# A planned list order that looks ahead on VectorE and ScalarE, and block sums issued in pieces

## The chip, the core and the metric

The kernel runs on one core of a Trainium2 chip. A core has TensorE (matrix products into the eight banks of PSUM, 128 partitions x 512 float32 each), VectorE and ScalarE (elementwise work, both can read and write PSUM), GpSimd, and SyncE, whose queue issues all DMAs of this kernel. The profile calls them PE (PEld for its weight loads), DVE, ACT, POOL and SP. The metric is the device time of one execution in microseconds; the time before is the median of three runs.

## The reference

Two blocks read the same normalised x. One is linear attention with 32 heads, the other a gated feed-forward net; the output is x plus the product of the first with silu of the second.

```python
def _A_ref(x, wqkv, wo):
    B, S, D = x.shape                # 1, 2048, 1024
    H = 32; Dh = D // H
    qkv = (lambda x, *d: x.transpose(*d))((x @ wqkv).reshape(B, S, 3, H, Dh), 2, 0, 3, 1, 4)
    q, k, v = qkv[0], qkv[1], qkv[2]
    phi = lambda t: jnp.where(t > 0, t + 1, jnp.exp(t)) + 1e-6
    pq, pk = phi(q), phi(k)
    kv = jnp.einsum("bhsd,bhse->bhde", pk, v)
    z = jnp.einsum("bhsd->bhd", pk)
    num = jnp.einsum("bhqd,bhde->bhqe", pq, kv)
    den = jnp.einsum("bhqd,bhd->bhq", pq, z)[..., None] + 1e-6
    o = num / den
    return (lambda x, *d: x.transpose(*d))(o, 0, 2, 1, 3).reshape(B, S, D) @ wo

def _B_ref(x, w_gate, w_up, w_down):
    g = _silu(x @ w_gate)            # w_gate, w_up: 1024 x 3584
    u = x @ w_up
    return (g * u) @ w_down

x = A_x
xn = _layernorm(x, axis=-1)
s = _A_ref(xn, A_wqkv, A_wo)
g = _silu(_B_ref(xn, B_w_gate, B_w_up, B_w_down))
return x + s * g
```

## The kernel before

**The products.** Nearly every product is a Strassen-Winograd product: the operands are cut into 2 x 2 blocks, and seven block products (numbered 1 to 7 in `Set.step`) do the work of eight. For that, sums and differences of blocks are needed on both sides. On the moving side they are called T1 = R01 - R00, T2 = R11 - T1, T3 = R11 - R01 and T4 = R10 - T2 (T1 is written over R01, so T3 comes first); products 5, 6, 7 and 4 read T1, T2, T3 and T4. On the stationary side the four sums are numbered 5, 6, 7 and 3. These block sums are VectorE subtractions of 16-bit data in SBUF, written with `tt(..., True)` (line 360). The change is about how they are cut:

- `combos` (line 459 on): T3, T1, T2, T4 of the weights for k and v (`KVV[0]`, `KVV[1]`) and of x (`XV[0]`, `XV[1]`), each one operation of 2048 elements a partition;
- `m_sum`: the same for the attention matrix `MV`, the four sums of 2048;
- `wd_sum`: T1 to T4 of the down weights, each as two halves of 3584;
- `Group.mk`: the sums of h in the down projection. There are four groups of 512 rows (`Group`). A group holds four blocks of h in slots of 14 pair blocks of 256 columns; `sum5`, `sum67` and `sum3` make four sums of them. Group 0 is loaded and summed in two cuts, pair blocks 0 to 11 and 12 to 13 (3072 and 512 elements), the others in one of 3584.

Around each step stand the evacuations: `put1` and `put5` copy a bank with ScalarE (`act`, line 350), products 6 and 7 add a copy to a bank with VectorE (line 360). `phi_evac` makes phi of a k or q block: the exponential on ScalarE, min and add on VectorE (L734, `tensor_scalar`), then max and add reading PSUM or SBUF (L735, `scalar_tensor_tensor`), which frees the bank.

**The stages.** First x is loaded, normalised by tile of 128 rows (`ln_tile`: statistics L647 and L651, aggregate L652, L653, a power on GpSimd L656, L664, then the scaled copy) and transposed. Tiles 0 and 1 go through `p_piece(tile, w, column half)`, plain products of eight matmuls of 512 columns with the weights of k (w = 0) and v (w = 1); three banks are held for kv sums and two for transposes in this time, so the pieces take turns in three banks. The order of the pieces is k of tile 0 (halves 1, 0), k of tile 1 (1, 0), v of tile 0 half 1, v of tile 1 half 1, v of tile 0 half 0, v of tile 1 half 0. Then come k and v of the other tiles as Strassen sets with the key-value sums (`a_tile`) in between; then q, gate and up by token half p = 0, 1 (`q_pair`, `gu_pair`), with the joint small products of products 1 and 5 cut once more (`inner_stat`, `inner_move`); the attention output (`s_pair`) between; h goes out to a scratch in DRAM (`h_done`); at last the down projection with h read back (`Group.load`), and the output.

**The order of the work** isn't written out: `Plan` collects every operation with its reads, writes, its cost in the plan and its preceding operations, and `schedule` makes a list order for each engine. Costs in the plan: an operation of VectorE takes its elements / 960 + 0.07 (16-bit: / 1920, some others more), so 0.603 for 1024 16-bit elements; a matmul of 512 columns 0.216; every result is there 0.25 to 0.3 us after its operation; a DMA has a rate and two fixed parts. An operation is due (`dl`) at what TensorE has to do before it in program order plus 30, or earlier, when a successor is due: its successor's due time less its own cost and latency. `schedule` plays this plan through: each engine that is free takes, of the operations that are ready in the plan, the one due first, or, where none is ready, the one that is ready first. TensorE takes the first in program order within a window of six. `emit` then writes each engine's list, with semaphore waits where a preceding operation is on another engine or on the same one (not for TensorE behind TensorE). On the chip each engine follows its list strictly: an operation whose data are late holds up all behind it.

Of the kernel before, what the change touches and what calls it, by code (L numbers as in the profile page):

```python
# [10 lines left out]
ALU = mybir.AluOpType  # L11
# [19 lines left out]
class Plan:  # L31
# [59 lines left out]
    def schedule(self):  # L91
        ops = self.ops
        for o in reversed(ops):
            d = o.pecum if o.eng == "pe" else o.pecum + 30.0
            for s in o.succs:
                extra = (4.0 + o.nbytes / 200e3) if o.sem is not None else o.busy + o.lat
                d = min(d, s.dl - extra)
            o.dl = d - o.urgent
        pes = [o for o in ops if o.eng == "pe"]
        cum = [o.pecum + o.busy for o in pes]  # L100
        for o in ops:
            if o.sem is not None and o.succs:
                k = bisect_right(cum, o.dl - self.lead) - 1
                if k >= 0 and pes[k] not in o.preds:
                    o.preds.add(pes[k])
                    pes[k].succs.append(o)
        for o in ops:
            o.npred = len(o.preds)
            o.ready = 0.0
        free = {e: 0.7 for e in self.ENGS}  # L110
        dma_free = 0.0
        table = ACT.Exp
        avail = {e: [] for e in self.ENGS}
        pe_next = deque(o for o in ops if o.eng == "pe")
        for o in ops:
            if o.npred == 0:
                avail[o.eng].append(o)
        order = []
        done = set()
        total = len(ops)  # L120
        while len(order) < total:
            best = None
            for e in self.ENGS:
                a = avail[e]
                if not a:
                    continue
                t = free[e]
                if e == "pe":
                    lim = None
                    n = 0  # L130
                    for o in pe_next:
                        if n >= self.window:
                            lim = o.idx
                            break
                        n += 1
                    cand = [o for o in a if lim is None or o.idx < lim]
                    if not cand:
                        continue
                    rdy = [o for o in cand if o.ready <= t + 0.05]
                    o = min(rdy, key=lambda o: o.idx) if rdy else min(cand, key=lambda o: (o.ready, o.idx))  # L140
                else:
                    rdy = [o for o in a if o.ready <= t]
                    o = min(rdy, key=lambda o: (o.dl - o.boost + self.SWITCH * (o.tab not in (None, table)), o.idx)
                            ) if rdy else min(a, key=lambda o: (o.ready, o.dl))
                s = max(t, o.ready)
                if best is None or s < best[0]:
                    best = (s, e, o)
            s, e, o = best
            o.start = s
            if o.sem is not None:  # L150
                free[e] = s + 0.08
                t0, rate, t1 = self.ALONE if o.start < self.RUSH else self.MIXED
                b = max(s + t0, dma_free)
                dma_free = b + o.nbytes / rate
                o.done = dma_free + t1
            else:
                busy = o.busy
                if o.tab not in (None, table):
                    table = o.tab
                    busy += self.SWITCH  # L160
                free[e] = s + busy
                o.done = s + busy + o.lat
            avail[e].remove(o)
            if e == "pe":
                done.add(o)
                while pe_next and pe_next[0] in done:
                    pe_next.popleft()
            order.append(o)
            for q in o.succs:
                q.npred -= 1  # L170
                q.ready = max(q.ready, o.done)
                if q.npred == 0:
                    avail[q.eng].append(q)
        self.order = order
        return order
# [55 lines left out]
def build_kernel(nc, A_x, A_wqkv, A_wo, B_w_gate, B_w_up, B_w_down, out, WINDOW=6, NWARM=14, NPE=4, LEAD=12.0):  # L231
# [12 lines left out]
    with ExitStack() as es:  # L244
# [98 lines left out]
        def nel(ap):  # L343
            n = 1
            for s in ap.shape[1:]:
                n *= s
            return n
# [8 lines left out]
        def dve(reads, writes, fn, n, rate=0.96):  # L356
            return PL.op("dve", reads, writes, fn, n / (rate * 1000.0) + 0.07)

        def tt(reads, writes, o, a, b, op, fast=False):
            return dve(reads, writes, lambda h: h.tensor_tensor(o, a, b, op), nel(o), 1.92 if fast else 0.96)  # L360
# [79 lines left out]
        def xview(arena, base=0):  # L440
            d = {}
            for nm, b in (("R00", 0), ("R10", 1), ("T1", 2), ("R11", 3), ("T2", 4), ("T3", 5), ("T4", 6)):
                d[nm] = xblock(arena, b, base)
            d["R01"] = d["T1"]
            return d

        XV = [xview(X), xview(P)]
        MV = xview(H, 16 * KB)

        def combos(v):  # L450
            tt([v["R11"][1], v["R01"][1]], [v["T3"][1]], v["T3"][0], v["R11"][0], v["R01"][0], ALU.subtract, True)
            tt([v["R01"][1], v["R00"][1]], [v["T1"][1]], v["T1"][0], v["R01"][0], v["R00"][0], ALU.subtract, True)
            tt([v["R11"][1], v["T1"][1]], [v["T2"][1]], v["T2"][0], v["R11"][0], v["T1"][0], ALU.subtract, True)
            tt([v["R10"][1], v["T2"][1]], [v["T4"][1]], v["T4"][0], v["R10"][0], v["T2"][0], ALU.subtract, True)


        wz = TM.at(0, 1 * KB, FP16)
# [2 lines left out]
        for n in range(NWARM):  # L460
            b = n % 8
# [207 lines left out]
        R01 = (H, 12 * KB)  # L669
# [173 lines left out]
        p_piece(0, 1, 1)  # L843
        t_tile(2)
        combos(KVV[0])
        p_piece(1, 1, 1)
        ln_tile(3)
        p_piece(0, 1, 0)
        t_tile(3)
        combos(KVV[1])  # L850
        p_piece(1, 1, 0)
        for b in tb:
# [50 lines left out]
        for q, kb in enumerate(kvb):  # L903
            n = 3 if q < 2 else 2
# [291 lines left out]
        MIN = {}  # L1196

        def m_sum(o, a, b):
            tt([MV[a][1], MV[b][1]], [MV[o][1]], MV[o][0], MV[a][0], MV[b][0], ALU.subtract, True)

        def s_pair(g):
            p, j0 = g // 2, g % 2
# [49 lines left out]
        def wv(nm, h):  # L1252
            vs, rs, _ = DV["T1" if nm == "R01" else nm]
            v = vs[h]
            return (v.bitcast(BF16) if nm[0] == "R" else v), rs[h]

        def wd_sum(o, a, b):
            for h in range(2):
                (ov, orr), (av, ar), (bv, br) = wv(o, h), wv(a, h), wv(b, h)
                tt([ar, br], [orr], ov, av, bv, ALU.subtract, True)  # L1260

        DIN = {}
        DAT = (tuple((W, q * 3584) for q in range(3)), ((W, 28 * KB), (W, 28 * KB + 3584), (W, 43 * KB)))
# [19 lines left out]
        def hv(s, n0=0, n1=NPAIR):  # L1283
            return (s.ap(FP16).rearrange("p (n t) -> p n t", t=256)[:, n0:n1], s.sub(n0 * 512, (n1 - n0) * 512).r)

        class Group:
# [11 lines left out]
                        h_scr[self.g, i, k][:, n0:n1, :], dsem("hl%d_%d" % (s.k, c)), (n1 - n0) * 64 * KB)  # L1298

            def mk(self, o, a, b, op):  # L1300
                for n0, n1 in self.cuts:
                    (ov, orr), (av, ar), (bv, br) = hv(o, n0, n1), hv(a, n0, n1), hv(b, n0, n1)
                    tt([ar, br], [orr], ov, av, bv, op, True)

# [58 lines left out]

        XV[1]["R01"] = xblock(R01[0], 0, R01[1])
        combos(XV[0])
        combos(XV[1])
        XIN[1] = inner_move(XV[1], 4, in_places(W, 6 * KB, KB))
# [28 lines left out]
        def s_first():  # L1396
            raw, cmb = raw_ring.take(), cmb_ring.take()
            for nm, (sl, o) in (("T2", (raw, 0)), ("T3", (raw, 4)), ("T4", (cmb, 0))):
                MV[nm] = xblock(sl.a, 0, sl.off + o * KB)
            m_sum("T2", "R11", "T1")  # L1400
            m_sum("T3", "T2", "R00")
            m_sum("T4", "R10", "T2")
            MIN.update(inner_move(MV, 4, (tuple((cmb.a, cmb.off + (4 + q) * KB) for q in range(3)),)))
            MIN.update(inner_move(MV, 4, (tuple((H, (40 + q) * KB) for q in range(3)),), ms=(5,)))
            sp[0] = s_pair(0)
# [36 lines left out]
        G[0].sum67()  # L1442
        feed(None)
        wd_sum("T2", "R11", "T1")
        wd_sum("T3", "T2", "R00")
        wd_sum("T4", "R10", "T2")
        for g, c in enumerate(G):
            n = G[g + 1] if g < 3 else None
# [73 lines left out]
def bass_recurrent_scan__linear_attn_block__swiglu_ffn__prompt_kernel(  # L1522
    nc: bass.Bass,
    A_x: bass.AP,
    A_wqkv: bass.AP,
    A_wo: bass.AP,
    B_x: bass.AP,
    B_w_gate: bass.AP,
    B_w_up: bass.AP,
    B_w_down: bass.AP,  # L1530
    out: bass.AP,
):
    build_kernel(nc, A_x, A_wqkv, A_wo, B_w_gate, B_w_up, B_w_down, out)
# [28 lines left out]
```

## Time and profile before

| | |
|---|---|
| median of 3 runs | 719.88 us (719.76 to 720.52) |
| the profiled execution's own time | 719.0 us |
| its span, first to last instruction | 717.2 us |
| granted TensorE clock | 1.00 in all parts |
| HBM read, written | 61.87 MB, 23.20 MB |

The times that follow are from the profiled execution and count from the start of its span. In a row of the timeline stand start, duration, engine, line, operation, what it writes and reads, and how often; in square brackets the idle time of the engine before it and what ended that. In a row of groups stand the number of operations, their busy time, the mean length of one in ns and the idle time before them. A row of waits has the total, the number and the longest in us. In a row of stretches stand its length and then the busy time (and number of instructions) of PE, PEld, DVE, ACT and POOL, the granted clock, the share of the DMA engines and GB/s. Neighbouring instructions of VectorE overlap by a little, so that durations add up to more than the time from start to start.

### The profile page before, as it was taken

The page shows a single profiled execution, that of the slowest core. Times are in us where ns is not written, and L with a number is a line of the kernel's source. Part 1 is how long each engine was busy: PE and PEld are TensorE (multiplying, and loading weights), DVE is VectorE, ACT ScalarE, POOL GpSimd, SP SyncE. Part 2 cuts the span into 40 slices and gives each one's busy share as a digit, 9 for nine tenths or more (in the row PEclk, how much of TensorE's full clock was granted, in tenths as well). Part 3 has the DMA queues.
Part 4 walks back from the last instruction along what each step waited for, and adds up shares of the span by engine and source line. Part 5 has one row for each costly group of instructions (what it writes and reads, how often), then busy time and mean ns, then how long its engine had stood idle before and what let it go on. Part 6 is the DMA issues. An engine that isn't in the chain of part 4 may idle for free.

```text
span 717.2 us, 10813 instructions
## 1 busy us (share of the span) xinstructions
PE 707.3 (99%) x4064; PEld 385.4 (54%) x4064; DVE 518.1 (72%) x1101; ACT 407.1 (57%) x785; POOL 14.3 (2%) x35
## 2 busy tenths in 40 slices
PE   7999999999999999999999999999999999999997
PEld 3444445555555555555555555555554465565643
DVE  5999896766966797678998355957659983737342
ACT  3766645777876686679966666565662122131211
POOL 2111100000000000000000000000000000000000
PEclk9999999999999999999999999999999999999999
DMA  9343223113211321264226227554336637353422
GB/s 309 102 90 88 52 67 118 60 60 101 75 60 60 117 79 44 78 201 138 89 74 190 96 82 237 189 177 165 114 123 223 234 119 235 127 181 125 135 65 83
DMA packets 86868, 88.92 MB, mean 124 GB/s; under 512 B 17440, under 2 KB 82720, under 8 KB 86816
## 3 DMA queue, kind: packets, MB, share of 16 engines
q1 hardware_dynamic: 86816, 88.23, 39.0%
q8 instruction: 32, 0.52, 0.3%
q14 instruction: 20, 0.16, 0.1%
HBM read 61.87 MB, written 23.20 MB: 119 GB/s over the span
## 4 chain that ended last, share of the span: by engine, by line
PE 95%; DVE 2%; DMA 1%; SPq 1%; ACT 0%; issue 0%
PE ps L220 95%; DMA H<-in_A_wqkv_dram 1%; SPq L363 1%; DVE H L360 1%; DVE H L735 0%; DVE stats L647 0%; DVE stats L651 0%; DVE TM L734 0%; PE ps L227 0%; DVE W L360 0%; DVE ps L360 0%; ACT W L350 0%; ACT TM L350 0%; ACT ps L350 0%; DVE TM L360 0%
## 5 line engine op out<-in xcount | busy, mean ns | idle before, releaser
L220 PE MATMUL ps<-P,W 128*128 128x512 f16 (+1 forms) x952 | 215.9, 350 | 0.0
L220 PE MATMUL ps<-X,W 128*128 128x512 f16 (+1 forms) x896 | 202.9, 350 | 0.0
L360 DVE TENSOR_TENSOR ps<-ps,TM 128x256 f32<-128x256 f32 (+1 forms) x246 | 129.6, 531 | 93.1 <-PE ps L220 65.2
L350 ACT ACTIVATE H<-ps 128x512 f16<-128x512 f32 (+2 forms) x225 | 133.3, 601 | 84.6 <-PE ps L220 84.1
L350 ACT ACTIVATE TM<-ps 128x512 f32<-128x512 f32 (+2 forms) x244 | 125.3, 531 | 33.1 <-PE ps L220 29.2
L220 PEld LDWEIGHTS ps<-P,W 128*128 128x128 f16 (+1 forms) x952 | 93.0, 98 | 74.2 <-ACT ps L350 0.3
L220 PEld LDWEIGHTS ps<-X,W 128*128 128x128 f16 (+1 forms) x896 | 87.4, 98 | 68.5 <-issue 0.2
L350 ACT ACTIVATE ps<-ps 128x512 f32<-128x512 f32 (+1 forms) x170 | 84.3, 496 | 59.5 <-PE ps L220 57.5
L360 DVE TENSOR_TENSOR W<-W 128x256 f16<-128x256 bf16 (+4 forms) x230 | 87.6, 418 | 27.1 <-ACT W L350 26.7
L360 DVE TENSOR_TENSOR H<-H 128x1024 f16<-128x1024 f16 (+6 forms) x124 | 84.0, 695 | 10.9 <-ACT H L350 8.0
L220 PE MATMUL ps<-H,X 128*128 128x512 bf16 (+3 forms) x388 | 82.4, 356 | 3.0 <-DVE H L735 1.0
L220 PE MATMUL ps<-W 128*128 128x256 f16 x444 | 78.6, 273 | 0.0
L220 PE MATMUL ps<-H,W 128*128 128x512 f16 (+3 forms) x370 | 76.9, 345 | 0.6 <-DVE W L360 0.3
L220 PE MATMUL ps<-H 128*128 128x512 bf16 (+4 forms) x418 | 75.3, 317 | 0.0
L220 PEld LDWEIGHTS ps<-W 128*128 128x128 f16 (+1 forms) x444 | 43.0, 98 | 29.3 <-ACT TM L350 1.4
L220 PEld LDWEIGHTS ps<-H,X 128*128 128x128 f16 x388 | 37.3, 98 | 38.8 <-DVE H L735 2.0
L360 DVE TENSOR_TENSOR TM<-ps,TM 128x512 f32<-128x512 f32 x59 | 40.5, 687 | 24.3 <-PE ps L220 24.3
L220 PEld LDWEIGHTS ps<-H 128*128 128x128 f16 (+1 forms) x418 | 37.0, 98 | 31.1
L220 PEld LDWEIGHTS ps<-H,W 128*128 128x128 f16 x370 | 35.5, 98 | 33.1 <-DVE W L360 1.1
L350 ACT ACTIVATE W<-ps 128x512 f16<-128x512 f32 x24 | 14.3, 597 | 56.4 <-PE ps L220 56.4
L360 DVE TENSOR_TENSOR H<-ps,TM 128x512 f16<-128x512 f32 (+1 forms) x35 | 24.0, 685 | 13.7 <-PE ps L220 13.7
L220 PE MATMUL ps<-W,H 128*128 128x512 f16 (+1 forms) x139 | 32.3, 368 | 0.0
(87 smaller groups left out, 453.8 us busy)
## 6 DMA issues: line engine op xcount, KB each, us to landing
h_scratch<-H SPq DMA_DIRECT2D x56, 256.0 KB, 2.2
W<-in_B_w_gate_dram SPq DMA_DIRECT2D x7, 1024.0 KB, 5.3
W<-in_B_w_up_dram SPq DMA_DIRECT2D x7, 1024.0 KB, 5.3
H<-in_B_w_down_dram SPq DMA_DIRECT2D x4, 1792.0 KB, 7.2
H<-h_scratch SPq DMA_DIRECT2D x7, 896.0 KB, 4.9
W<-in_A_x_dram SPq DMA_DIRECT2D x16, 256.0 KB, 3.2
H<-in_A_wqkv_dram SPq DMA_DIRECT2D x8, 512.0 KB, 8.2
H<-r_scratch SPq DMA_DIRECT2D x32, 128.0 KB, 3.0
```

The costliest lines, as they stand in the source:

```text
L220: last = h.matmul(o, l, r, start=st, stop=sp, skip_group_check=True)
L350: op = PL.op("act", reads, writes, lambda h: h.activation(o, i, func, **kw), nel(o) / 1200.0 + (0.055 if src == "ps" else 0.095))
L360: return dve(reads, writes, lambda h: h.tensor_tensor(o, a, b, op), nel(o), 1.92 if fast else 0.96)
L363: return PL.op("sp", reads, writes, lambda h: h.dma_start(o, i), 0.08, sem=s, nbytes=nbytes, cow=cow, after=after)
```

## The change

In `schedule`, an engine other than TensorE that is free at t still picks the ready operation o that is due first. If o is no DMA, it now looks at the operations whose predecessors are all planned and that become ready within half of o's cost after t. Those that are due more than 8 us earlier than o count; of them the one that is ready first, u, is looked at. If some ready operation fits in before u is ready (with 0.05 to spare), the one of those due first is taken; otherwise the engine is kept for u. Beside that, the sums of `combos`, `m_sum`, `wd_sum` and `Group.mk` are issued in pieces with regions of their own: two halves, three parts (1024, 1024 and 1536 elements) of each half, and cuts of 4, 4, 4 and 2 pair blocks. The loads of h keep their cuts.

```diff
--- before.py
+++ after.py
@@ -140,8 +140,17 @@
                     o = min(rdy, key=lambda o: o.idx) if rdy else min(cand, key=lambda o: (o.ready, o.idx))
                 else:
                     rdy = [o for o in a if o.ready <= t]
-                    o = min(rdy, key=lambda o: (o.dl - o.boost + self.SWITCH * (o.tab not in (None, table)), o.idx)
-                            ) if rdy else min(a, key=lambda o: (o.ready, o.dl))
+                    rank = lambda o: (o.dl - o.boost + self.SWITCH * (o.tab not in (None, table)), o.idx)
+                    if not rdy:
+                        o = min(a, key=lambda o: (o.ready, o.dl))
+                    else:
+                        o = min(rdy, key=rank)
+                        if o.sem is None:
+                            soon = [u for u in a if t < u.ready < t + 0.5 * o.busy and rank(u)[0] + 8 < rank(o)[0]]
+                            if soon:
+                                u = min(soon, key=lambda u: u.ready)
+                                fit = [x for x in rdy if t + x.busy <= u.ready + 0.05]
+                                o = min(fit, key=rank) if fit else u
                 s = max(t, o.ready)
                 if best is None or s < best[0]:
                     best = (s, e, o)
@@ -447,11 +456,22 @@
         XV = [xview(X), xview(P)]
         MV = xview(H, 16 * KB)
 
+        def piece(b, q, n=2):
+
+            ap, r = b
+            keys, m = r.keys, len(r.keys) // n
+            return ap[:, 4 // n * q:4 // n * q + 4 // n, :], Region(keys[m * q:m * q + m])
+
+        def block_sub(v, o, a, b):
+            for q in range(2):
+                (oa, orr), (aa, ar), (ba, br) = (piece(v[nm], q) for nm in (o, a, b))
+                tt([ar, br], [orr], oa, aa, ba, ALU.subtract, True)
+
         def combos(v):
-            tt([v["R11"][1], v["R01"][1]], [v["T3"][1]], v["T3"][0], v["R11"][0], v["R01"][0], ALU.subtract, True)
-            tt([v["R01"][1], v["R00"][1]], [v["T1"][1]], v["T1"][0], v["R01"][0], v["R00"][0], ALU.subtract, True)
-            tt([v["R11"][1], v["T1"][1]], [v["T2"][1]], v["T2"][0], v["R11"][0], v["T1"][0], ALU.subtract, True)
-            tt([v["R10"][1], v["T2"][1]], [v["T4"][1]], v["T4"][0], v["R10"][0], v["T2"][0], ALU.subtract, True)
+            block_sub(v, "T3", "R11", "R01")
+            block_sub(v, "T1", "R01", "R00")
+            block_sub(v, "T2", "R11", "T1")
+            block_sub(v, "T4", "R10", "T2")
 
 
         wz = TM.at(0, 1 * KB, FP16)
@@ -1196,7 +1216,7 @@
         MIN = {}
 
         def m_sum(o, a, b):
-            tt([MV[a][1], MV[b][1]], [MV[o][1]], MV[o][0], MV[a][0], MV[b][0], ALU.subtract, True)
+            block_sub(MV, o, a, b)
 
         def s_pair(g):
             p, j0 = g // 2, g % 2
@@ -1256,8 +1276,10 @@
 
         def wd_sum(o, a, b):
             for h in range(2):
-                (ov, orr), (av, ar), (bv, br) = wv(o, h), wv(a, h), wv(b, h)
-                tt([ar, br], [orr], ov, av, bv, ALU.subtract, True)
+                for n0, n1 in ((0, 2), (2, 4), (4, 7)):
+                    (ov, orr), (av, ar), (bv, br) = ((v[:, n0:n1], Region(r.keys[4 * n0:4 * n1]))
+                                                     for v, r in (wv(nm, h) for nm in (o, a, b)))
+                    tt([ar, br], [orr], ov, av, bv, ALU.subtract, True)
 
         DIN = {}
         DAT = (tuple((W, q * 3584) for q in range(3)), ((W, 28 * KB), (W, 28 * KB + 3584), (W, 43 * KB)))
@@ -1298,7 +1320,7 @@
                         h_scr[self.g, i, k][:, n0:n1, :], dsem("hl%d_%d" % (s.k, c)), (n1 - n0) * 64 * KB)
 
             def mk(self, o, a, b, op):
-                for n0, n1 in self.cuts:
+                for n0, n1 in ((0, 4), (4, 8), (8, 12), (12, 14)):
                     (ov, orr), (av, ar), (bv, br) = hv(o, n0, n1), hv(a, n0, n1), hv(b, n0, n1)
                     tt([ar, br], [orr], ov, av, bv, op, True)
 
```

## The prediction

> **What bounds the kernel now.** I read the head of the page and the chain of waits first, to see which engine sets the end.
>
> ```profile
> span 717.2 us, 10813 instructions
> PE 707.3 (99%) x4064; PEld 385.4 (54%) x4064; DVE 518.1 (72%) x1101; ACT 407.1 (57%) x785; POOL 14.3 (2%) x35
> PE ps L220 95%; DMA H<-in_A_wqkv_dram 1%; SPq L363 1%; DVE H L360 1%; DVE H L735 0%; DVE stats L647 0%; DVE stats L651 0%; DVE TM L734 0%; PE ps L227 0%; DVE W L360 0%; DVE ps L360 0%; ACT W L350 0%; ACT TM L350 0%; ACT ps L350 0%; DVE TM L360 0%
> ```
>
> TensorE is busy for 707.3 of 717.2 us and holds 95% of the chain that ended last. The change adds and removes no matmul, so only the 9.9 us outside that figure, and what the modelled ends hide, can move. The waits of TensorE alone say where it stood still.
>
> ```profile
> PE ps L220 <- POOL ident L403: 1.4, 1, 1.4
> PE ps L220 <- DVE H L735: 1.0, 2, 0.8
> PE ps L220 <- DMA H<-in_A_wqkv_dram: 1.0, 1, 1.0
> PE ps L220 <- ACT X L350: 0.5, 1, 0.5
> PE ps L220 <- DVE veps L653: 0.5, 1, 0.5
> PE ps L220 <- DVE W L360: 0.3, 1, 0.3
> PE ps L220 <- DVE ps L360: 0.3, 1, 0.3
> ```
>
> That is 5.0 us in eight waits. The rest of the 9.9 us, 4.9 us, is the end: the last elementwise operation starts at 713.43 and its output still has to be stored.
>
> ```profile
> 704.59 4.70 PE L220 MATMUL ps<-H 128*128 128x512 bf16 x21
> ...
> 713.43 0.42 DVE L360 TENSOR_TENSOR TM<-W,TM 128x512 bf16<-128x512 f16 x1
> L220 PE MATMUL ps<-H,P 128*128 128x512 bf16 (+1 forms) x80 | 19.5, 379 | 0.0
> ```
>
> The first and third of these rows size a wait properly. One matmul of 512 columns is drawn 0.379 us long, but 21 of them take 4.70 us, so they start (4.70 - 0.379) / 20 = 0.216 us apart. A wait printed as x therefore costs TensorE x + 0.379 - 0.216 = x + 0.163 us.
>
> Waits for the identity, for a load and for the first transposed x (1.4, 1.0 and 0.5) do not hang on the order of VectorE. Five waits do: two on L735 (0.8 and 0.28 below), the one put down to L653, the one on ps L360 and the one on W L360. They cost 0.76 + 0.28 + 0.46 + 0.29 + 0.34 + 5 x 0.163 = 2.95 us. That, 0.4% of the span, is all that a better order can win; 51.3 to 559 us and everything after 562 us show no wait of TensorE at all and can only lose.
>
> **The change part by part.** Three of the waits lie in the first 21 us.
>
> ```profile
> 13.50 0.62 ACT L350 ACTIVATE TM<-ps 128x512 f16<-128x512 f32 x1
> ...
> 14.99 2.76 PE L220 MATMUL ps<-H,X 128*128 128x512 bf16 x12 [0.76 <-DVE H L735]
> 15.28 1.23 DVE L360 TENSOR_TENSOR H<-H 128x2048 f16<-128x2048 bf16 x1 [0.35 <-DMA H<-in_A_wqkv_dram]
> 16.42 0.29 DVE L734 TENSOR_SCALAR TM<-TM 128x512 f16<-128x512 f16 x1
> ...
> 17.30 0.68 DVE L735 SCALAR_TENSOR_TENSOR H<-ps,TM 128x512 bf16<-128x512 f32 x1
> 17.89 0.69 DVE L651 BATCH_NORM_STATS2 stats<-W 128x6 f32<-128x512 bf16 x1
> 18.03 1.04 PE L220 MATMUL ps<-H,X 128*128 128x512 bf16 x4 [0.28 <-DVE H L735]
> 18.49 1.21 DVE L360 TENSOR_TENSOR H<-H 128x2048 f16<-128x2048 bf16 x1
> 19.61 0.29 DVE L734 TENSOR_SCALAR TM<-TM 128x512 f16<-128x512 f16 x1
> ...
> 20.09 0.69 DVE L735 SCALAR_TENSOR_TENSOR H<-ps,TM 128x512 bf16<-128x512 f32 x1
> ...
> 20.84 3.63 PE L220 MATMUL ps<-H,X 128*128 128x512 bf16 x16 [0.46 <-DVE veps L653]
> ```
>
> Five of the eight PSUM banks are held at this time, so the projection pieces turn over three banks, and a bank comes free when L735 has read it. The exponential that L734 needs was done at 13.50 + 0.62 = 14.12, yet L734 ran at 16.42, behind a block sum that waited for its own weights until 15.28 and then took 1.23 us. The planner put them in that order because in its plan the sum's data come earlier. TensorE stood until that L735 ended (17.98 against 18.03). The second sum, at 18.49, does the same to the L734 at 19.61; I read the wait at 20.84 as one for the L735 that ends at 20.78, since L653 feeds no matmul directly.
>
> The split alone lets L734 in after one half. Half of a sum of 2048 elements has 1024, and the forms show both:
>
> ```profile
> L360 DVE TENSOR_TENSOR H<-H 128x1024 f16<-128x1024 f16 x72 | 48.7, 686 | 7.0 <-ACT H L350 7.0
> L360 DVE TENSOR_TENSOR H<-H 128x2048 f16<-128x2048 bf16 x8 | 9.7, 1219 | 2.0 <-DMA H<-in_A_wqkv_dram 2.0
> L360 DVE TENSOR_TENSOR P<-H 128x3584 f16<-128x3584 bf16 x2 | 4.0, 2022 | 0.2 <-PE ps L220 0.2
> ```
>
> A half is 1.219 - 0.686 = 0.53 us shorter, so L734 and L735 can come 0.53 us earlier, at both places. That covers the whole of the first wait (0.28 + 0.163 = 0.44) and most of the second (0.46 + 0.163 = 0.62). The look-ahead goes the same way at the first place. By the planner's own arithmetic in the code (14 warm-ups of 0.38, transposes of 0.448, pieces of 1.728) the bank in question is wanted at 13.13, so L735 is due at 13.13 - 0.603 - 0.3 = 12.22 and L734 at 12.22 - 0.501 = 11.72; the sum at 15.28, which I read as T3 of the value weights, since it waits for a load and those of the key weights were asked for earlier, is due in halves two halves (2 x 0.903) ahead of the first matmul that reads T1, at 26.57 of TensorE work: 24.76. The gap of 13 exceeds 8, and the rule would hold VectorE for L734 if that comes ready within 0.30 of a half's start. At the second place T1 of the key weights is due near 20.9 and L734 near 13.9: under 8, so only the split helps. I take 0.35 of 0.44 and 0.35 of 0.62, because L734 must be next in the new order as well; the bounds are 0 and 1.0 for both together. The wait at 14.99 I leave: the work ahead of that L735 is the statistics of the next tile, due at 10.36 by the same arithmetic against 10.0 for L734, so neither edit moves it (bounds 0 to 0.92).
>
> The next is at 51.29.
>
> ```profile
> 49.34 0.69 DVE L651 BATCH_NORM_STATS2 stats<-W 128x6 f32<-128x512 bf16 x1
> ...
> 49.95 0.68 DVE L735 SCALAR_TENSOR_TENSOR H<-TM 128x512 bf16<-128x512 f32 x1
> ...
> 50.54 0.69 DVE L360 TENSOR_TENSOR ps<-ps,TM 128x512 f32<-128x512 f32 x1
> ...
> 51.29 2.76 PE L220 MATMUL ps<-H,W 128*128 128x512 f16 x12 [0.29 <-DVE ps L360]
> ```
>
> The sum in PSUM that TensorE waits for starts at 50.54, after statistics and an evacuation that reads SBUF and holds no bank. Nothing here is split; only the look-ahead can turn the last two round, if the sum became ready in the plan within 0.30 of the start of the 0.60 us evacuation. It became ready somewhere in that time, or it would have gone first: one half. I take half of 0.29 + 0.163, 0.23; bounds 0 and 0.45.
>
> The last is at 559.17.
>
> ```profile
> 552.28 1.75 DVE L360 TENSOR_TENSOR X<-X 128x3072 f16<-128x3072 f16 x1
> 553.95 2.02 DVE L360 TENSOR_TENSOR P<-P,H 128x3584 f16<-128x3584 f16 x1
> 555.89 2.89 DVE L360 TENSOR_TENSOR H<-H 128x1024 f16<-128x1024 f16 x4
> 558.70 0.42 DVE L360 TENSOR_TENSOR W<-X 128x512 f16<-128x512 f16 x1
> L360 DVE TENSOR_TENSOR W<-H 128x1792 f16<-128x1792 bf16 x2 | 2.2, 1083 | 0.0
> ```
>
> Pair blocks 12 and 13 of group 0's first h sum (558.70) are what the down projection waits for. In front of them stand four operations whose results are wanted tens of microseconds later: products h of the other token half, and, as 2.89 us is more than four of 0.6, a sum of 1792 elements for the next group's small products. The plan took the load for later than that. The rank condition holds (far more than 8), and the window before the 1.0 us operation is half of it: again one half of 0.34 + 0.163, 0.25; bounds 0 and 0.50.
>
> **What is added** lies on VectorE alone: no DMA, since the loads keep their cuts. Twenty sums of 2048 (eight on the k and v weights, eight on x, four on the attention matrix) become forty: 20 more. Eight halves of down weights become 24: 16 more. Four sums of group 0 go from two to four pieces, twelve of the other groups from one to four: 8 + 36 more. Together 80. By durations a split 2048 costs 2 x 0.686 - 1.219 = 0.153; a 3584 in three, with 0.95 for 1536 between the rows of 1024 and 2048, costs 0.30; a 3584 in four (with 0.42 for the 512) 0.46; the 3072 in three 0.31. That gives 20 x 0.153 + 8 x 0.30 + 12 x 0.46 + 4 x 0.31 = 12.2 us. But neighbours overlap: L735 at 17.30 takes 0.68 and the next starts at 17.89, the 2048 at 18.49 takes 1.21 and the next starts at 19.61, so each gives back about 0.09, and the 80 cost 12.2 - 80 x 0.09 = 5.0 us. I take 5.0, as these rows are of the same queue.
>
> [...]
>
> What hides the 5.0 us, and where it is tight:
>
> ```profile
> 45.00:50.00 5.00, 5.00 (x31) 2.52 (x30) 3.77 (x13) 3.97 (x7) 1.06 (x2) 1.00 0.90 157
> 545.00:560.00 15.00, 14.66 (x69) 6.48 (x67) 15.00 (x13) 3.55 (x6) 0.00 (x0) 1.00 0.52 162
> 560.00:580.00 20.00, 20.00 (x101) 9.77 (x100) 20.00 (x27) 3.68 (x7) 0.00 (x0) 1.00 0.51 182
> 580.00:600.00 20.00, 20.00 (x133) 12.76 (x132) 10.74 (x19) 4.24 (x8) 0.00 (x0) 1.00 0.51 169
> ```
>
> The third figure of a row is VectorE. Early, the eight splits of weights add 8 x (0.153 - 0.09) = 0.5 us, and 1.2 us of idle time at 45 to 50 takes them up. From 545 to 580 VectorE is full, and five halves of down weights, three sums of group 0 and one of group 1 fall there: 5 x 0.30 + 3 x 0.31 + 0.46 = 2.9 us by durations, less 19 more instructions x 0.09 = 1.2 us by starts. The 1792s (1.08 each, eight of them under several names) are due a group later and can move into 580 to 600, where 9.3 us are free. I cost the additions at 0.3 us of new waits (bounds 0 and 2.9).
>
> Sum: -0.35 - 0.35 - 0.23 - 0.25 + 0.3 = -0.9 us. The profiled execution took 719.0 us, 1.8 more than its span, and the median of three runs is 719.88, 0.9 above the profiled one. Against 719.0 that makes 718.1, at the median 719.0.
>
> **The rivals.** *Everything lands*: both early waits go whole (1.06), the two coin flips fall well (0.95), nothing is lost: 2.0 us, 717.9. For it: the split helps the early two without the look-ahead. Against it: four hits at once.
>
> *A full VectorE from 545 to 580 passes its extra work on*: slower. The s5, s6, T2, T3 chain has more instructions and the due evacuations queue behind them. It decides when the planner lets less than 1.2 us of low-priority work slide behind 580; then TensorE waits for 1.2 to 2.9 us, 721.1 to 722.8, and a hold that the rule puts into a full stretch adds to that. For it: 20.00 of 20.00 busy. Against it: no wait of TensorE there after 559.17.
>
> *The order doesn't do what it says*: the planner's plan misjudges landings (a load meant earlier came at 15.28), so holds and halves land beside the real waits, and all stays at 719.9.
>
> **How the numbers follow.** Forecast (718.3 to 719.6) 0.42; everything lands 0.20; slower 0.22; nothing moves 0.16. A measurement of this kernel tells about 0.2%, 1.44 us, from no change. Faster than 718.44: the second case and the lower edge of the first, 0.25. Slower than 721.32: the third case, most of it, 0.21. The rest is 0.54. The range goes from 717.5, below everything landing, to 721.5, the lower part of the slower case.
>
> **What would show it.** Right: VectorE has about 1181 instructions and TensorE 707 us; L734 starts about half a microsecond after the sum at 15.3 begins to run, the waits near 18.0 and 20.8 shrink, and those near 51 and 559 are gone or unchanged. Wrong: any new wait of TensorE between 60 and 712 us, above all at 545 to 580, or a wait near 14.99 that goes as well.

## The result and the profile after

The changed kernel takes 717.34 us (median of 7 runs, 716.80 to 718.07) beside 719.69 us for the kernel before (7 runs): ratio 0.9967, 95% interval 0.9955 to 0.9978. That is 2.35 us less. The prediction said 719.0 and a range down to 717.5: the sign was right, the gain came out more than two and a half times as large. The profiled execution took 716.87 us, 2.13 less than that of before. One of the ten executions of the kernel that looks ahead from 130 us on took 1256.94 us at a granted clock of 0.557; its figures below are of the other nine.

The head of the page of the changed kernel:

```profile
span 715.1 us, 10861 instructions
PE 705.0 (99%) x4035; PEld 385.8 (54%) x4064; DVE 528.0 (74%) x1181; ACT 407.4 (57%) x785; POOL 13.7 (2%) x35
```

VectorE has its 80 more instructions, and its busy time is up by 9.9 us. Not all of that is theirs: the look-ahead alone (below) has a busy time of 522.3 us with 1101 instructions, 4.2 more than before with none added, and the pieces alone have 524.2 us with 1181. So the 80 cost 5.7 us beside the look-ahead and 6.1 without it, 0.07 to 0.08 us each; the rest comes with the new order. TensorE's 4064 weight loads are all there; of its matmuls 29 records are missing, so its 705.0 us is no saving, and a gap of exactly one matmul in its rows is a lost record, not a wait.

The waits of TensorE in the changed kernel (engine and line, waited for what: total us, times, longest). Its line 229 is line 220 of before, 369 is 360, 359 is 350, 754 and 755 are 734 and 735, 667 and 671 are 647 and 651:

```profile
PE ps L229 <- POOL ident L412: 1.4, 1, 1.4
PE ps L229 <- DVE nmean L684: 0.9, 1, 0.9
PE ps L229 <- DMA H<-in_A_wqkv_dram: 0.7, 1, 0.7
PE ps L229 <- ACT X L359: 0.5, 1, 0.5
PE ps L229 <- ACT ps L359: 0.2, 1, 0.2
```

Of the five waits that hung on VectorE's order one is left, at 14.71; the waits at 18.0, 20.8, 51.3 and 559.2 are gone, and one on a copy by ScalarE is new. What happened at the first places, from the timeline of the changed kernel:

```profile
12.94 0.55 PEld L229 LDWEIGHTS ps<-H,X 128*128 128x128 f16 x4 [0.36 <-ACT X L359]
...
14.64 0.29 DVE L754 TENSOR_SCALAR TM<-TM 128x512 f16<-128x512 f16 x1
14.71 3.14 PEld L229 LDWEIGHTS ps<-H,X 128*128 128x128 f16 x16 [1.22 <-DVE H L755]
...
14.96 0.69 DVE L755 SCALAR_TENSOR_TENSOR H<-ps,TM 128x512 bf16<-128x512 f32 x1
15.70 0.69 DVE L667 BATCH_NORM_STATS2 stats<-W 128x6 f32<-128x512 bf16 x1
16.31 0.68 DVE L671 BATCH_NORM_STATS2 stats<-W 128x6 f32<-128x512 bf16 x1
16.90 0.68 DVE L369 TENSOR_TENSOR H<-H 128x1024 f16<-128x1024 bf16 x1
17.49 0.29 DVE L754 TENSOR_SCALAR TM<-TM 128x512 f16<-128x512 f16 x1
```

Before, the block sum at 15.28 stood ahead of L734 and L735, which ran at 16.42 and 17.30. Now the pair runs at 14.64 and 14.96 and the first half of any block sum only at 16.90, so L735 is 2.3 us earlier, not the half sum (0.53) that the prediction gave it. (The half at 16.90 is of the sum that stood at 18.49; by the list that the planner's code makes, the one from 15.28 comes from 23.89 on.) The weight loads show that the wait at 14.71 itself did not change, whatever the matmul rows say: idle 1.22 here, and in the kernel before

```profile
14.98 0.98 PEld L220 LDWEIGHTS ps<-H,X 128*128 128x128 f16 x6 [1.25 <-DVE H L735]
```

The place of the old wait at 51.3, in the changed kernel:

```profile
48.53 0.63 PE L229 MATMUL ps<-H 128*128 128x129 bf16 x8
48.73 0.70 DVE L369 TENSOR_TENSOR ps<-ps,TM 128x512 f32<-128x512 f32 x1 [0.19 <-PE ps L229]
...
51.87 0.69 DVE L667 BATCH_NORM_STATS2 stats<-W 128x6 f32<-128x512 bf16 x1
```

The sum in PSUM is next in VectorE's list, which stands idle for 0.19 us until TensorE has its data; the statistics that went ahead of the sum before (at 49.34) come only at 51.87. The idle time looks like a hold of the new rule, but the planner's code decides on none here: in the plan's own time, in which this sum starts at 49.0, its nearest holds are at 14.6 and 49.8 us, and the list at this place is another because the plan ahead of it is. The place of the old wait at 559:

```profile
553.16 1.29 DVE L369 TENSOR_TENSOR H<-H 128x1024 f16<-128x1024 f16 x2
554.36 0.42 DVE L369 TENSOR_TENSOR W<-X 128x512 f16<-128x512 f16 x1
...
555.50 0.69 DVE L369 TENSOR_TENSOR H<-H 128x1024 f16<-128x1024 f16 x1
555.62 3.18 PE L229 MATMUL ps<-H,W 128*128 128x512 f16 x14
```

The due sum of 512 comes 4.3 us earlier than in the profile before, more than the 1.5 us or so that the list had won by then, ahead of work that stood in front of it there, and TensorE, whose own list is another here too, has no wait. Here again the planner has no hold: this sum is planned for 555.8, the holds around it for 542.1 and 556.2, and it goes when a piece of 1024 ends. The new wait:

```profile
35.99 0.63 PE L229 MATMUL ps<-H 128*128 128x129 bf16 x8
36.12 0.70 DVE L369 TENSOR_TENSOR ps<-ps,TM 128x512 f32<-128x512 f32 x1
36.19 0.58 ACT L359 ACTIVATE ps<-ps 128x512 f32<-128x512 f32 x1 [0.63 <-PE ps L229]
...
36.83 1.04 PE L229 MATMUL ps<-H,X 128*128 128x512 bf16 x4 [0.20 <-ACT ps L359]
```

TensorE runs out of other work while ScalarE copies a bank: 0.20 + 0.163 = 0.36 us. And the stretch that the slower rival spoke of, with VectorE in the third figure after the length:

```profile
545.00:560.00 15.00, 14.95 (x70) 6.82 (x70) 14.67 (x25) 2.96 (x5) 0.00 (x0) 1.00 0.54 171
560.00:580.00 20.00, 19.89 (x103) 10.10 (x104) 19.52 (x33) 3.08 (x6) 0.00 (x0) 1.00 0.48 183
580.00:600.00 20.00, 19.89 (x127) 12.45 (x128) 12.14 (x25) 4.84 (x9) 0.00 (x0) 1.00 0.49 163
```

VectorE does 1.4 us more than before between 580 and 600, and TensorE has no wait in these rows beyond lost records.

### The profile page after: what moved, and what is told of

It reads as the page before. It is cut to its first block, busy times and chain, and to the rows that moved or that the text cites. A ratio compares the mean times of both kernels' runs of the same rounds, so it can differ in the third digit from the quotient of the medians.

```text
span 715.1 us, 10861 instructions
## 1 busy us (share of the span) xinstructions
PE 705.0 (99%) x4035; PEld 385.8 (54%) x4064; DVE 528.0 (74%) x1181; ACT 407.4 (57%) x785; POOL 13.7 (2%) x35
## 4 chain that ended last, share of the span: by engine, by line
PE 97%; DMA 1%; DVE 0%; SPq 0%; issue 0%; ACT 0%
PE ps L229 97%; DMA W<-in_A_x_dram 1%; SPq L372 0%; PE ps L236 0%; DVE stats L667 0%; DVE H L755 0%; ACT W L359 0%; DVE stats L671 0%; ACT ps L359 0%; DVE W L369 0%; DVE TM L369 0%; DVE mv L672 0%; DVE TM L754 0%; DVE veps L673 0%; DVE nmean L684 0%
## 5 line engine op out<-in xcount | busy, mean ns | idle before, releaser
L369 DVE TENSOR_TENSOR H<-H 128x1024 f16<-128x1024 f16 (+3 forms) x143 | 85.7, 622 | 12.8 <-ACT H L359 8.1
L229 PE MATMUL ps<-H,X 128*128 128x512 bf16 (+3 forms) x376 | 80.0, 355 | 2.9 <-DVE nmean L684 0.9
L229 PE MATMUL ps<-H 128*128 128x129 bf16 (+4 forms) x407 | 73.4, 315 | 0.4
L229 PEld LDWEIGHTS ps<-H,X 128*128 128x128 f16 x388 | 37.3, 98 | 37.5 <-DVE H L755 1.2
```

What stands on the lines that cost most here:

```text
L229: last = h.matmul(o, l, r, start=st, stop=sp, skip_group_check=True)
```

## The experiments

Two terms moved whatever the kernel: from one execution to the next the wait for the first weights (1.00 and 0.5 us in the two profiles of before, 0.70 and 0.82 in the two of the changed kernel), and from session to session the median of before (719.7, 720.4, 719.7, 719.6 in the four sessions). A wait of the transposes at 7.1 to 7.4 us came and went as well, and the wait for the first weights took it up: it was 1.14 us in the changed kernel's second profile and not there in its first, and the weights ended their wait at 10.09 and 9.86. So each kernel is read in two ways: by its ratio to before on the same chip, and by the waits of TensorE in its profile. The table has the waits that hang on the order, printed idle time plus 0.163; "-" is no wait. The one at 14.7 (0.9 in all kernels but those with late banks) is left out.

| kernel | at 18.0 | 20.8 | 51.3 | 559 | new | ratio to before, 95% |
|---|---|---|---|---|---|---|
| before | 0.44 | 0.62 | 0.45 | 0.50 | | |
| before again | 0.45 | 0.61 | 0.45 | 0.50 | | |
| changed | - | - | - | - | 0.36 at 36.8 | 0.9967 (0.9955 to 0.9978) |
| look-ahead alone | - | - | - | - | 0.36 at 37.5 | 0.9970 (0.9958 to 0.9981) |
| pieces alone | - | 0.41 | 0.48 | - | 0.37 at 97.5, 1.13 at 104.8 | 0.9997 (0.9988 to 1.0006) |
| look-ahead before 20 us | - | - | 0.36 | 0.50 | 0.36 at 37.3 | 0.9983 (0.9974 to 0.9993) |
| 20 to 130 us | 0.40 | 0.61 | - | 0.50 | 0.67 at 98.1 | 1.0001 (0.9992 to 1.0011) |
| from 130 us | 0.45 | 0.61 | 0.95 | - | | 0.9988 (0.9978 to 0.9997) |

**The look-ahead alone** (all sums whole, as before):

```diff
-            block_sub(v, "T3", "R11", "R01")
+            tt([v["R11"][1], v["R01"][1]], [v["T3"][1]], v["T3"][0], v["R11"][0], v["R01"][0], ALU.subtract, True)
...
-                for n0, n1 in ((0, 4), (4, 8), (8, 12), (12, 14)):
+                for n0, n1 in self.cuts:
```

> The block sums whole again, the look-ahead kept. The changed kernel lost four waits of TensorE that the kernel before has: near 18.0 (0.44 us with the 0.163 of the modelled end), 20.8 (0.62), 51.3 (0.45) and 559.2 us (0.50), 2.0 us together, and won one near 36.4 (0.37). Theory (look-ahead and pieces each end some of them): the waits at 18.0 and 51.3 are gone here, those at 20.8 and 559 stay; time about 0.9 us under before, 718.8. Rival A (the look-ahead does it all): all four gone, 717.5 or less. Rival B (the pieces do it all): all four stay, 719.7.

718.12 us beside 720.42, ratio 0.9970. All four waits are gone; rival A, with the look-ahead doing it all, is what the profile shows. Rows of its waits, without the identity and the first weights:

```profile
PE ps L229 <- DVE nmean L673: 1.0, 1, 1.0
PE ps L229 <- ACT X L359: 0.5, 1, 0.5
PE ps L236 <- DVE veps L662: 0.5, 1, 0.5
PE ps L229 <- ACT ps L359: 0.2, 1, 0.2
```

The last is the new wait, here with no sum cut: the look-ahead brings it without the pieces. (The wait on nmean is the one at 14.7, that on veps one of the transposes.)

**The pieces alone** (the selection of the old scheduler):

```diff
-                        if o.sem is None:
-                            soon = [u for u in a if t < u.ready < t + 0.5 * o.busy and rank(u)[0] + 8 < rank(o)[0]]
...
```

> The rule of the scheduler as before, the block sums in pieces. Theory (each ends some): the waits at 20.8 and 559 go or shrink, the one at 51.3 stays (nothing near it is cut), the one at 18.0 shrinks at most; about 1.1 us under before, 718.6. Rival A (the look-ahead does it all): all four stay and the 80 extra instructions cost VectorE 5 to 12 us of which some shows, 719.7 or more. Rival B: all four gone, 717.4.

720.07 us beside 720.42, ratio 0.9997: no gain that can be told from none. The pieces do what the prediction said of them at the start (18.0 gone, 20.8 from 0.62 to 0.41) and end the wait at 559, but two new waits between 97 and 105 us take more than that back:

```profile
102.80 0.69 DVE L360 TENSOR_TENSOR P<-P 128x1024 f16<-128x1024 f16 x1
...
103.40 0.69 DVE L746 SCALAR_TENSOR_TENSOR H<-TM 128x512 bf16<-128x512 f32 x1
104.00 0.70 DVE L360 TENSOR_TENSOR ps<-ps,TM 128x512 f32<-128x512 f32 x1
...
104.75 2.76 PE L220 MATMUL ps<-H,W 128*128 128x512 f16 x11 [0.97 <-DVE ps L360]
```

The sum in PSUM that TensorE wants (L360 on ps) comes behind a half of a sum of x and an evacuation from SBUF: the old fault at another place.

**Sums of the down stage whole**, all else as changed:

```diff
-                for n0, n1 in ((0, 2), (2, 4), (4, 7)):
+                for n0, n1 in ((0, 7),):
...
-                for n0, n1 in ((0, 4), (4, 8), (8, 12), (12, 14)):
+                for n0, n1 in self.cuts:
```

> Of the changed kernel, the sums of the down weights and of h whole again (as before), everything else kept. If the cuts of the down stage end the wait at 559, it is back here: TensorE waits 0.3 to 0.5 us between 540 and 570, and the time is 0.5 us over the changed kernel, 717.8. If the look-ahead or the shift of the stage ends it, no wait there and the time is that of the changed kernel, 717.3.

717.67 us beside 720.42, ratio 0.9963 (0.9950 to 0.9976), no wait between 540 and 570. The 60 instructions that the down stage got (16 for the weights, 44 for h) make no difference that can be told beside the look-ahead.

**Is the order of before stable?** The kernel before once more:

> The kernel before once more, for its waits. The first profile had TensorE waits that VectorE's order ends at 18.0, 20.8, 51.3 and 559.2 us. If they belong to the order, they stand here at the same work and with 0.3 to 0.6 us each, whatever the first loads do; if they come from late loads at the start, the first three differ by more than 0.3 us or are missing.

One execution, 718.77 us. All five waits stand again within 0.02 us, while TensorE waited 0.5 us for the first weights and not 1.0.

**The look-ahead in parts** (whole sums; the plan's time t limited):

```diff
-                        if o.sem is None:
+                        if o.sem is None and t < 20.0:
```

and `20.0 <= t < 130.0`, `t >= 130.0` in the other two.

> Whole block sums; the look-ahead acts only for operations that the plan places before 20 us. Theory: the waits at 18.0 and 20.8 are gone (1.06 us), those at 51 and 559 stay as far as the list there is still the old one; 718.7 to 719.0 against 719.9. Rival (the gain is one of a shifted plan as a whole): all four gone or none.

718.65 us beside 719.70. As the theory said: 18.0 and 20.8 gone, 559 untouched. The wait near 51 is there, but now on ScalarE, and the new wait at 37.3 comes with this part. Its rows, without the identity, the first weights and the transposes:

```profile
PE ps L229 <- DVE H L744: 0.8, 1, 0.8
PE ps L229 <- ACT X L359: 0.5, 1, 0.5
PE ps L229 <- ACT ps L359: 0.4, 2, 0.2
PE ps L229 <- DVE W L369: 0.3, 1, 0.3
```

The planner's code makes three holds in this part, all at the first place: for the small operation L673, and for L743 and L744 (L734 and L735 of before). What they do at the second place is seen in the timeline:

```profile
17.36 1.21 DVE L369 TENSOR_TENSOR H<-H 128x2048 f16<-128x2048 bf16 x1
...
18.96 0.68 DVE L744 SCALAR_TENSOR_TENSOR H<-ps,TM 128x512 bf16<-128x512 f32 x1
...
22.79 1.22 DVE L369 TENSOR_TENSOR H<-H 128x2048 f16<-128x2048 bf16 x1
```

Before, two sums of 2048 ran ahead of this evacuation, at 15.28 and 18.49, and it started at 20.09. Here one does: the sum that was put off at the first place is out of the way at the second.

> Whole block sums; the look-ahead acts only on operations placed from 20 to 130 us. Theory: the wait at 51.3 is gone (0.45 us) and those at 18.0 and 20.8 stay; the wait near 36 that the changed kernel has is absent, as no hold lies ahead of it; 719.4. Rival: the wait at 51.3 stays, or 18.0 and 20.8 go too.

719.66 us beside 719.70. The wait at 51.3 is gone, the others stay, as expected; what was not expected is a wait at 98.1 that eats it:

```profile
98.14 1.90 PE L229 MATMUL ps<-H,W 128*128 128x512 f16 x8 [0.51 <-DVE ps L369]
```

The sums of x are whole here, so a wait at this place does not need the pieces. At 51.3 the planner keeps VectorE, in place of the statistics, for the L743 right ahead of the due sum.

> Whole block sums; the look-ahead acts only on operations placed at or after 130 us. Theory: only the wait at 559 is gone (0.50 us); those at 18.0, 20.8 and 51.3 stay; 719.4. Rival (that wait goes by the shift of the early part): it stays.

718.92 us beside 719.70. The wait at 559 is gone by the holds after 130 us alone. Its timeline shows the step that the prediction took for a coin flip, the due 512 ahead of the sum of 1792, for which the planner holds VectorE here:

```profile
556.38 1.90 DVE L369 TENSOR_TENSOR H<-H 128x1024 f16<-128x1024 f16 x3
558.18 0.43 DVE L369 TENSOR_TENSOR W<-X 128x512 f16<-128x512 f16 x1
...
559.33 1.08 DVE L369 TENSOR_TENSOR H<-H 128x1792 f16<-128x1792 bf16 x1
```

This run also has the wait near 51 at twice its size, with the lists of all engines the same as before up to 133 us:

```profile
48.45 0.70 DVE L656 BATCH_NORM_STATS2 stats<-W 128x6 f32<-128x512 bf16 x1 [0.40 <-DMA W<-in_A_x_dram]
...
51.04 0.69 DVE L369 TENSOR_TENSOR ps<-ps,TM 128x512 f32<-128x512 f32 x1
...
51.79 2.76 PE L229 MATMUL ps<-H,W 128*128 128x512 f16 x12 [0.79 <-DVE ps L369]
```

A tile of x landed late, the statistics at the head of VectorE's list waited 0.40 us for it, and the due sum behind them started at 51.04, where the profile of before has 50.54. So that wait of the old list, 0.45 us in two executions of the kernel before, was 0.95 us in this one with its late load. The medians differ by 0.78, though the waits of this profile come to no gain: 0.50 won at 559, 0.50 lost to the late tile.

**TensorE's own list.** The rule leaves TensorE out, but its order follows the plan: in the changed kernel another weight load, by tile names and shape, stands at 336 of the 4064 places of its list, among them the stretch from 541 to 577 us. That its new order ends the waits is a rival, and the parts speak against it: with the look-ahead before 20 us alone TensorE's list is that of the kernel before up to 32 us, with 20 to 130 us alone up to 63, and with 130 us on alone from 491 us to the end. The waits at 18.0, 20.8, 51.3 and 559 go there all the same.

**The wait that is left at 14.7**: the banks of the kv sums are taken after the plain pieces, not ahead of them.

```diff
-        kvb = [balloc_part() for _ in range(3)]
+        kvb = []
...
         for b in tb:
             bfree(b)
+        kvb.extend(balloc_part() for _ in range(3))
```

> Of the changed kernel, the three banks of the kv sums are taken only after the plain pieces of tiles 0 and 1, so that these turn over six banks and not three. The wait that is left at 14.7 us (0.95 printed, 1.11 with the modelled end) is put down to a bank that VectorE frees late. Theory (it is the bank): it shrinks by most of its 1.1 us, 716.3 to 716.6, unless x of the next tile comes too late to use the time. Rival (it is the data: x of tile 1 or the weights arrive only then): the wait stays and the time is 717.3.

717.70 us beside 720.42, ratio 0.9966 (0.9955 to 0.9978); its profile caught an execution of 719.03 us in which TensorE waited 1.85 us for the first weights. So it ran again, beside the changed kernel on one chip:

> The changed kernel once more, beside the next three on one chip. Its list order has two waits of TensorE that hang on other engines' order (14.7 us: 0.92 by the weight loads; 36.8 us: 0.37); both should stand again, at the same work, while the wait for the first weights varies by some 0.3 us or more from execution to execution. Ratio to before 0.9967 as first measured; a rival that the first result was a lucky chip would give 0.999 or more.

> The banks of the kv sums taken late, again: its one profiled execution had the latest weights of all (TensorE waited 2.0 us for them) and so could not tell whether the 0.92 us that the bank wait cost are won. If they are, it is 0.5 to 1.2 us faster than the changed kernel on the same chip (the wait at 36.8 is gone too). If the loads take the time over, it is within 0.3 us of it, and the profile has longer waits for weights and x at the start.

The changed kernel 717.57 us, ratio to before (719.59) 0.9975 (0.9964 to 0.9986), with the same two waits; with late banks 717.00, ratio 0.9966 (0.9954 to 0.9979). Its waits of TensorE:

```profile
PE ps L229 <- POOL ident L412: 1.4, 1, 1.4
PE ps L229 <- DMA H<-in_A_wqkv_dram: 1.3, 2, 0.8
PE ps L229 <- ACT X L359: 0.5, 1, 0.5
```

The wait at 14.7 is gone, so a bank it was, and the one at 36.8 is gone with it. Of the 0.92 us a second wait for weights takes 0.45 + 0.163 = 0.61 back, at 13.79. The median is 0.57 us lower, but the intervals of the two ratios overlap: the lowest median of its session, not a settled gain.

**A window of the whole cost**, `t + 1.0 * o.busy` for `t + 0.5 * o.busy`:

> The changed kernel with a window of the whole cost of the operation in place of half. If a half window still leaves due operations behind longer ones, waits that are left shrink (36.8) and the time falls by 0.2 to 0.5 us. If the half already caught what matters and longer holds only leave VectorE idle, the time is the same or up to 1 us longer, with new waits between 20 and 110 us, where VectorE is busiest.

717.13 us, ratio 0.9970 (0.9958 to 0.9981), the same waits as the changed kernel: a hold twice as long ends none of those that are left.

**Look-ahead, whole sums and late banks:**

> Look-ahead, whole block sums, banks of the kv sums taken late. If the pieces bring nothing beside the look-ahead, it equals e10 within 0.4 us; if the pieces are what lets due operations in early, it is 0.5 us or more over e10 and shows waits near 20 or 104 us.

718.60 us, ratio 0.9988 (0.9979 to 0.9997), 1.6 us over the version with pieces, though the two intervals just touch. The profile has the later weights of a slow start (1.84 us) and three waits that the version with pieces lacks, 1.59 us together:

```profile
27.64 1.04 PE L229 MATMUL ps<-H,W 128*128 128x512 f16 x4 [0.38 <-DVE veps L662]
32.25 1.90 PE L229 MATMUL ps<-H,W 128*128 128x512 f16 x8 [0.52 <-DVE ps L369]
39.14 1.04 PE L229 MATMUL ps<-H,X 128*128 128x512 bf16 x4 [0.20 <-ACT ps L359]
```

So the pieces are not without use in every list; whether they or the accident of this list make the difference was not tried apart.

## Why the prediction was right or wrong

**The bound held.** Five waits of 2.95 us together were the most that the order could win; 2.35 was won, and the second profile of before has the same five.

**The two early waits: mechanism half right, size too small.** The prediction let L734 in behind a half of the sum and took 0.35 of each. The pieces alone do just that: they end the first wait and take 0.21 us off the second. In the changed kernel the whole sum goes behind the pair, by the hold that the prediction described but gave no weight of its own, and both waits end: 1.06 us for 0.70. At the second place it reckoned that the rule could not act (a gap under 8). No hold does act there; the wait goes because the sum that was held back at the first place no longer runs ahead of the second. The prediction took what stands ahead of each wait as given. (Its dues at the first place, 12.22, 11.72 and 24.76, are 9.68, 9.17 and 22.46 in the planner's figures, with the same gap of 13; the sum at 18.49 is T3 of the key weights there, not T1.)

**The waits at 51.3 and 559: the step that failed most.** Each was taken at half its cost, 0.23 and 0.25, as a mean over a yes and a no that had no basis but ignorance. Both came out as yes, 0.45 and 0.50, and either is ended by holds in its own part of the plan alone. A mean of two such terms is a time that no list has; the two outcomes, all or nothing, belonged into the range, and the case of all, priced at 2.0 us, got only 0.20. The coin need not have been thrown either: the planner is code, and its plan of the kernel before has the figures. At 559 the sum of 1792 is planned for 559.41 and the due 512 is ready at 559.66, inside the window of half a microsecond: a hold. At 51.3 the prediction asked the wrong pair: the sum in PSUM is ready in the plan (49.05) before the evacuation starts (49.61) and goes second only because it is due 0.5 us later, so no hold can turn these two round. What a hold can put off is the statistics, planned for 49.01 and due 15 us later than the sum, and in the run that looks ahead from 20 to 130 us that is what it does. In the changed kernel itself both waits are gone without a hold at their place, by the changed list ahead of them, which the prediction had no term for.

**The wait at 14.99**: left alone by both edits, as said (idle of the weight loads 1.25 and 1.22).

**The additions.** Durations were to add 12.2 us and starts 5.0, and the prediction took the starts; the 5.7 and 6.1 us of busy time for the 80 pieces bear it out. All of it was covered, at 545 to 580 too, so the slower rival did not come. The 0.3 us set aside for new waits met 0.36, but of another cause: not the pieces' work, as the look-ahead alone has it.

**The sum.** By the waits, the gain is 1.06 + 0.45 + 0.50 - 0.36 = 1.65 us where 0.9 was forecast. The profiled executions differ by 2.13, of which about 0.25 is a sooner first weight (TensorE waits 0.7 for it and not 1.0). Counted off one by one against those of before, the weight loads of the changed kernel are ahead by 0.25 us at 12 us, 1.36 at 21, 0.98 at 43, 1.44 at 52, 1.54 at 149 and 2.06 from 611 us to the end: steps at the named waits, and 0.16 us in steps too small to be printed as waits. So the profiles are accounted for; the medians are not in full. They differ by 2.35, and by 717.57 against 719.59 in the later session, 2.02. One way in which the old list can lose more than in its profile is shown above: its wait at 51 grew from 0.45 to 0.95 when a tile of x was late. How often that happens was not measured.

**The low end of the range**, 717.5, was set 0.4 us under the case of everything landing, less than before's own runs spread (719.31 to 720.52); the measured median lies 0.16 below it.

## What to carry to other kernels

In a kernel whose bound engine is busy for 99%, list its waits one by one: their sum is the most that an order can win. Where a wait goes or stays whole, price the outcomes, not their mean, and where the order is made by code, print the plan before pricing it. A rule that keeps an engine for a due operation about to be ready can pay where cutting the long operations does not; here it ended all four waits without the cuts, and the cuts alone moved the wait to another place. When two parts of a planned list are changed, neither acts by itself: judge them by single parts, and look for a wait that appears a few stages later.

## What the runs showed of the hardware

Two halves that followed each other took VectorE little longer than the whole: the pair of 1024 elements at 553.16 took 1.29 us from first start to last end, where one operation of 2048 took 1.22. The whole read bfloat16 and the pair float16; single operations of 1024 took 0.683 us from bfloat16 and 0.686 from float16. And the time to the first weights differed between executions of one list: the first wait for them was 1.85 us in one profile of the kernel with late banks and 0.84 in the other, a difference of 1.0 us beside the 2.35 that the change won.
